# Attention products from block 6 on as 64x64 matmuls on the four quarters of TensorE's array, k and v loaded by head, orders written anew

## The chip, the cores and the metric

The kernel runs on one core of a Trainium2 chip. The metric is the device time of one execution in microseconds. Three runs of the kernel before took 210.29, 210.59 and 211.29 us; the median is 210.59 us.

## The reference

A chunked linear attention with a decay per head is followed by a feed-forward layer with a "snake" activation. There are 4 batches, 8 heads, 768 positions and 64 values per head; the feed-forward layer takes 3072 tokens of 512 values through 2048 hidden values. Cut to what matters:

```python
for b in range(nb):                                   # nb = 12 blocks of 64 positions
    intra = einsum('bhic,bhjc->bhij', qb, kb) * Dmask # Dmask[i,j] = lam**(i-j) for i >= j, else 0
    intra = einsum('bhij,bhjd->bhid', intra, vb)
    inter = einsum('bhid,bhde->bhie', qb * lam**(pos+1), kv_state)
    out[:, :, sl] = intra + inter
    kv_state = lam**64 * kv_state + einsum('bhsd,bhse->bhde', kb * lam**(63-pos), vb)
h = x @ w_in                                          # x: tokens x (heads * 64)
g = h + sin(alpha * h)**2 / (alpha + 1e-9)
return g @ w_out
```

## The kernel before

**Blocks.** The kernel works with 24 blocks of 128 positions, six to a batch (s = 0 to 23, n = s % 6). Decay is put into the operands: q is multiplied by lam to the position and k by lam to minus the position (scale_block, L460 to L501), so that one mask of ones and zeros is left for the products within a block, and the state of a batch is a plain running sum. Four blocks make a chunk c of 512 tokens of the feed-forward layer (xT[c], 6 chunks).

**One block of attention.** With two heads to a pair of 128 partitions, a block has four products on TensorE (PE): S, the scores of its keys and queries (part_S, L618); Z, the sum of k times v, which is accumulated in PSUM bank 7 over the whole batch (part_Z, L662 from block 6 on); the part of the output that comes from the state of earlier blocks (L713 for blocks 6 to 11, whose copy Zc holds the state alone; L700 for the others, whose copy Zd is block-diagonal and 128 by 128); and the output from the masked scores (L722). DVE masks the scores out of two banks into Sm (L629). ACT or DVE copies the state to Zc or Zd (L678, L672) and the output to xT (L732). piece_G(s, t) (L806) issues S of block s and the output and Z of block t as one piece of PE work. Blocks 0 to 3 use other functions (piece_P, piece_I).

**Inputs of a block.** load_kv (L351) loads k and v of one block with one DMA each, 128 positions on 128 partitions, all 8 heads, 256 KB; load_q (L327) loads q for two blocks, 512 KB. All are issued by SP. scale_block then makes bf16 copies (qk2, v2). For blocks below 8, PE transposes q and k (L516, L539); from block 8 on a DMA transpose does (L506), which SP issues too.

**Feed-forward.** unit_A (L828) and unit_A2 (L862) are the first product, one bank of 512 columns at a time; ACT takes the sine (L838, L872), POOL or ACT squares it (L843, L842), DVE adds (L845, L880) into gT. The second product is unit_B (L893) for chunk 0, and from chunk 1 on unit_P (L981), seven half-size products with sums of weights and tokens (L936, L959).

**What sets the order.** Every operation is recorded with an index and with what it reads and writes. A table written out by hand, _Plan.ORDER, gives for each engine (PE, ACT, DVE, POOL, SP) the indices in the order in which that engine runs them; an operation that may run on several engines runs on the one whose table holds it. Semaphore waits follow from the reads and writes. Every engine runs its list strictly in order.

Of the kernel before, what the change touches and what calls it, by code (L numbers as in the profile page):

```python
# [5 lines left out]
ALU = mybir.AluOpType  # L6
# [29 lines left out]
class _Plan:  # L36
# [16 lines left out]
        ),  # L53
        "ACT": (
# [161 lines left out]
def bass_lightning_attn__then__act_snake_kernel(  # L216
# [16 lines left out]
    NBLK = B * NB  # L233
    NM = DFF // 128
    NKC = DM // 128
    TCH = 512
    NCH = B * S // TCH
    BPC = TCH // BL

    RL = 6  # L240
    R2 = 6
    RT = 6
    TD = 8
    LB = 12
    SD = 12
# [12 lines left out]
    with es:  # L258
# [54 lines left out]
        def _(_unused_eng):  # L313
# [322 lines left out]
            def diag(s):  # L636
                return s < NB or s >= SD

# [616 lines left out]
```

## Time and profile before

| | |
|---|---|
| median of three runs | 210.59 us |
| span of the profiled execution, first to last instruction | 208.2 us |
| TensorE matmuls busy | 200.0 us, 96% |
| DVE, ACT, POOL busy | 168.5, 147.7, 132.4 us |
| moved by DMA | 34.40 MB in 83222 packets, 59632 of them under 512 B |

The page doesn't tell how long the profiled execution took outside its span. Beside the median of the runs, the span leaves 2.4 us for what lies ahead of the first and behind the last instruction. The chain of work that ended last lies to 79% on PE.

### The profile page before, as it was taken

What the parts mean: (1) busy time and instruction counts of PE and PEld (TensorE: products, weight loads), DVE (VectorE), ACT (ScalarE), POOL (GpSimd) and SP (SyncE); (2) the same over time, 40 slices, a digit from 0 to 9 for tenths busy, and PEclk for the clock granted to TensorE, in tenths of its full rate; (3) what the DMA queues carried; (4) which work ended last, traced back from release to release, by engine and by line L of the source; (5) the groups of instructions that cost most, each with busy time, mean ns of one, the idle gap of its engine ahead of it and who ended that gap; (6) DMA issues with size and microseconds to landing.
All of it is one profiled execution on the core that took longest, in us unless ns stands there. A gap on an engine that the chain in (4) does not pass through costs nothing.

```text
span 208.2 us, 4897 instructions
## 1 busy us (share of the span) xinstructions
PE 200.0 (96%) x1972; PEld 136.8 (66%) x1972; DVE 168.5 (81%) x296; ACT 147.7 (71%) x270; POOL 132.4 (64%) x140
## 2 busy tenths in 40 slices
PE   6988999999997999998999999999999999999995
PEld 6756444557765877665657576665667666667994
DVE  2898567886989999987988979899798866767854
ACT  5658999448998999976979776898765579734300
POOL 6065689834968987954796850958851695585400
DMA  4999999999899999799997999380300004000324
GB/s 133 323 315 216 202 255 214 213 238 245 197 179 230 232 250 248 154 215 206 208 245 156 242 271 185 67 194 26 136 0 3 0 32 169 3 0 20 128 94 165
DMA packets 83222, 34.40 MB, mean 165 GB/s; under 512 B 59632, under 2 KB 80384, under 8 KB 83200
## 3 DMA queue, kind: packets, MB, share of 16 engines
q1 hardware_dynamic: 78544, 29.24, 62.5%
q0 software_dynamic: 3696, 3.67, 10.9%
q10 hardware_dynamic: 960, 1.19, 1.9%
q8 instruction: 15, 0.25, 0.5%
q14 instruction: 7, 0.06, 0.1%
HBM read 27.28 MB, written 6.29 MB: 161 GB/s over the span
## 4 chain that ended last, share of the span: by engine, by line
PE 79%; DVE 9%; ACT 4%; DMA 3%; SPq 2%; issue 1%; ACTq 1%; POOL 0%
PE bank L828 28%; PE bank L981 26%; PE bank L862 7%; PE bank L893 6%; PE bank L722 3%; PE bank L618 3%; DMA v<-in_v_dram 3%; SPq L324 2%; DVE gT L880 2%; DVE Sm L629 2%; DVE gT L845 2%; PE bank L700 1%; DVE w L936 1%; PE bank L654 1%; ACT Zd L672 1%; PE bank L662 1%
## 5 line engine op out<-in xcount | busy, mean ns | idle before, releaser
L828 PE MATMUL bank<-xT,w 128*128 128x512 bf16 x296 | 70.9, 380 | 1.0 <-ACT kept L1018 0.7
L845 DVE SCALAR_TENSOR_TENSOR gT<-u,rinv,bank 128x512 bf16<-128x512 bf16 x74 | 53.6, 744 | 18.2 <-ACT u L842 14.1
L838 ACT ACTIVATE t<-bank,alpha 128x512 bf16<-128x512 f32 x74 | 49.9, 683 | 19.9 <-PE bank L828 19.0
L828 PEld LDWEIGHTS bank<-xT,w 128*128 128x128 bf16 x296 | 27.8, 98 | 28.8 <-DVE gT L845 1.4
L959 POOL TENSOR_TENSOR gT<-gT 128x512 bf16<-128x512 bf16 x28 | 32.1, 1158 | 14.1 <-DVE Xs L959 8.9
L842 ACT ACTIVATE u<-t 128x512 bf16<-128x512 bf16 x57 | 35.2, 628 | 1.5
L843 POOL TENSOR_TENSOR u<-t 128x512 bf16<-128x512 bf16 x17 | 17.6, 1040 | 25.7 <-ACT t L838 25.7
L629 DVE TENSOR_TENSOR Sm<-bank,mask 128x1024 bf16<-128x1024 f32 x24 | 28.9, 1216 | 3.0 <-PE bank L618 1.1
L862 PE MATMUL bank<-xT,w 128*128 128x256 bf16 x176 | 21.6, 273 | 1.0 <-DVE gT L880 1.0
L880 DVE SCALAR_TENSOR_TENSOR gT<-u,rinv,bank 128x256 bf16<-128x256 bf16 x44 | 18.9, 474 | 4.2 <-ACT u L876 3.5
L959 POOL TENSOR_TENSOR Xs<-gT 128x512 bf16<-128x512 bf16 x19 | 21.8, 1162 | 0.3 <-DVE gT L845 0.3
L981 PE MATMUL bank<-w,gT 128*128 128x256 bf16 (+1 forms) x168 | 20.1, 268 | 0.0
L872 ACT ACTIVATE t<-bank,alpha 128x256 bf16<-128x256 f32 x44 | 18.5, 471 | 2.0 <-PE bank L862 1.7
L981 PE MATMUL bank<-ws,gT 128*128 128x256 bf16 x160 | 19.6, 273 | 0.0
L981 PE MATMUL bank<-w,Xs 128*128 128x256 bf16 (+1 forms) x168 | 19.5, 268 | 0.0
L478 POOL TENSOR_TENSOR qk<-q,Lq 128x512 bf16<-128x512 f32 x17 | 18.2, 1077 | 2.0 <-DMA q<-in_q_dram 2.0
L497 POOL TENSOR_TENSOR qk<-k,Lk 128x512 bf16<-128x512 f32 x16 | 17.4, 1090 | 3.3 <-DMA k<-in_k_dram 3.2
L862 PEld LDWEIGHTS bank<-xT,w 128*128 128x128 bf16 x176 | 16.3, 98 | 4.2 <-DVE gT L880 1.8
L981 PEld LDWEIGHTS bank<-w,gT 128*128 128x128 bf16 x168 | 15.9, 98 | 4.1 <-DVE gT L959 0.2
L981 PEld LDWEIGHTS bank<-w,Xs 128*128 128x128 bf16 x168 | 15.6, 98 | 3.3
L981 PEld LDWEIGHTS bank<-ws,gT 128*128 128x128 bf16 x160 | 15.3, 98 | 3.1 <-ACT xT L732 0.4
L893 PE MATMUL bank<-w,gT 128*128 128x512 bf16 x64 | 15.8, 380 | 0.0
(105 smaller groups left out, 266.0 us busy)
## 6 DMA issues: line engine op xcount, KB each, us to landing
k<-in_k_dram SPq DMA_DIRECT2D x24, 256.0 KB, 5.1
q<-in_q_dram SPq DMA_DIRECT2D x12, 512.0 KB, 6.2
v<-in_v_dram SPq DMA_DIRECT2D x24, 256.0 KB, 5.8
out_dram<-osb SPq DMA_DIRECT2D x18, 256.0 KB, 2.6
w<-in_moe_w_out_dram POOLq DMA_DIRECT2D x4, 512.0 KB, 7.8
w<-in_moe_w_in_dram POOLq DMA_DIRECT2D x3, 512.0 KB, 8.1
ws<-in_moe_w_in_dram SPq DMA_DIRECT2D x2, 512.0 KB, 7.5
out_dram<-osb ACTq DMA_DIRECT2D x8, 128.0 KB, 3.7
```

Of the source, the lines that this page charges most:

```text
L478: lambda e, a=a: e.tensor_tensor(qk2[:, j:j + 2, 4 * a:4 * a + 4, :], q32[:, jq, 4 * a:4 * a + 4, :, :].rearrange("p h t d -> p t h d"), b ...
L629: op("DVE", lambda e: e.tensor_tensor(Sm[js][:, :, :], banks[:, 512 * b0:512 * b0 + 1024].rearrange("p (c i) -> p c i", i=128), bass.AP(ma ...
L828: ins = e.matmul(ps[hb][:, c0:c1], w1[:, kc, 128 * m:128 * (m + 1)], xT[x][:, kc, c0:c1], start=(kc == 0 and c0 == lo), stop=(kc == NKC - ...
L838: op("ACT", lambda e: e.activation(t16[ju][:, w], ps[hb][:, w], ACTF.Sin, scale=alpha[:, m:m + 1]), 0.69 if hi - lo == TCH else 0.475, [ba ...
L842: lambda e: (e.activation(u16[ju][:, w], t16[ju][:, w], ACTF.Square) if e is nc.scalar else e.tensor_tensor(u16[ju][:, w], t16[ju][:, w], ...
L845: op("DVE", lambda e: e.scalar_tensor_tensor(out=gT[g][:, m, w], in0=u16[ju][:, w], scalar=rinv[:, m:m + 1], in1=ps[hb][:, w], op0=ALU.mul ...
L862: ins = e.matmul(ps[hb][:, 256 * i:256 * i + 256], w1[:, kc, 128 * (m + i):128 * (m + i + 1)], xT[x][:, kc, lo:lo + 256], start=(kc == 0 a ...
L872: op("ACT", lambda e, i=i: e.activation(t16[ju][:, 256 * i:256 * i + 256], ps[hb][:, 256 * i:256 * i + 256], ACTF.Sin, scale=alpha[:, m + ...
L880: op("DVE", lambda e, i=i: e.scalar_tensor_tensor(out=gT[g][:, m + i, lo:lo + 256], in0=u16[ju][:, 256 * i:256 * i + 256], scalar=rinv[:, ...
L893: ins = e.matmul(ps[ob][:, w], gT[g][:, m, 128 * s4:128 * (s4 + 1)], w2[:, m, w], start=(m == 0), stop=(m == NM - 1),)
L959: e.tensor_tensor(dst, in0, in1, alu), 0, rd, wr))
L981: ins = e.matmul(ps[ob][:, lo + d0:lo + d1], lhs, rhs[:, d0:d1], start=first and p == 0, stop=(p == NM // 2 - 1), skip_group_check=True)
```

## The change

**Products.** From block 6 on (NL = 6) piece_G calls a new function, quarters(s, t, ob), in place of part_S, part_O and part_Z. Every matmul in it has 64 rows and 64 columns of weights. The four quarters of the array are named by the half of the partitions that a matmul reads (rows) and the half of the partitions of PSUM that it writes (columns); four matmuls that follow each other go to four different quarters. Keys are cut into two halves of 64 positions; the second half meets only the second 64 queries, so its matmuls have 64 columns in place of 128.

Up to three pieces of PE work come out of one call. The first ("begun") is half of the product with the state. The second ("mid") is the scores of block s and the state's new term of block t. The third ("end") is the rest of the product with the state and the output of block t. Scores and the state's term lie in banks 1 and 2, the output in banks 7 and ob, one for each half of rows.

**Around the products.** The state is no longer kept in PSUM: DVE adds each block's term to an fp32 copy in SBUF (Zs), and ACT, DVE or POOL casts that to Zc. The masked scores have 768 columns in place of 1024, with a mask of their own (mlate). The output goes to xT in two copies of 256 columns in place of one of 512.

**Loads.** From block 6 on, k and v come by head: a DMA for three blocks of one head, 64 positions on 64 partitions, 6 times 64 values each (96 KB); heads 0, 1, 4 and 5 lie on the lower half of the partitions, the others on the upper half. The factors of k (Lk) are made anew for that layout, with two iotas and two small multiplies more at the start; the new mask takes four affine selects.

**Orders.** All five tables of ORDER are new; of PE's, a line before and after:

```diff
-            235, 244, 225, 236, 240, 251, 264, 248, 249, 272, 320, 257, 283, 278, 270, 293, 321, 289, 308, 302,
+            254, 269, 280, 277, 278, 293, 301, 286, 356, 312, 299, 307, 325, 357, 318, 319, 344, 338, 350, 331,
```

```diff
+    NL = 6
-    SD = 12
...
             def load_kv(s, which="kv"):
                 b, n, j = s // NB, s % NB, s % RL
                 for nm, src, dst in (("k32", k, k32), ("v32", v, v32)):
-                    if nm[0] not in which or (s < NP and s % 2):
+                    if nm[0] not in which or (s < NP and s % 2) or (s >= NL and s % 3):
                         continue
...
+                    for h in range(H):
+                        half, jp, par = h // 4, h // 2 % 2, h % 2
+                        at = H * D * j + D * (2 * par + half)
+                        load(
+                            bass.AP(dst, 64 * jp * RL * H * D + at, [[RL * H * D, 64], [4 * D, 6], [1, D]]),
+                            src[b, h, n * BL:(n + 3) * BL, :].rearrange("(c p) d -> p c d", p=64),
+                            [(nm, j + i, h) for i in range(3)], 0.45, f"{nm}{j}u", lat=1.5,
+                        )
...
+            def quarters(s, t, ob):
+                xy = (XB, ob)
+                n = 0 if t is None else t % NB
...
+                def inter(e, same):
...
+                    for par in range(2):
+                        for half in range(2):
+                            jp = half if same else 1 - half
+                            ins = mm(e, ("o", jp), half, par,
+                                     ps[xy[jp]][rows(par), 128 * half:128 * half + 128].rearrange("p (t x) -> p t x", t=2),
+                                     Zc[(t - 1) % 2][rows(half), 2 * jp + par, :], qkT[rows(half), jq:jq + 2, 2 * jp + par, u])
...
+                def scores(e):
...
+                    for c in range(2):
+                        x = slice(u.start + 32 * c, u.stop)
+                        for par in range(2):
+                            at = 640 + 192 * par + 64 * (1 - c)
+                            for half, jp in ((0, 0), (1, 1), (0, 1), (1, 0)):
...
+                def state(e):
...
+                    for c in range(2):
+                        for par in range(2):
+                            for jp, half in ((0, 0), (1, 1), (0, 1), (1, 0)):
+                                i = 4 * c + 2 * par + half
+                                lo = 512 + 896 * jp + 64 * par
+                                ins = mm(e, ("s", jp), jp, half, banks[rows(half), lo:lo + 64],
+                                         qk2[rows(jp), j, H + i, :], v2[rows(jp), j, i, :])
...
+                def outputs(e):
...
+                    for c in range(2):
+                        for half in range(2):
+                            for jp, par in ((0, 0), (1, 1), (0, 1), (1, 0)):
...
+                if t is not None and n:
+                    begun = op("PE", lambda e: inter(e, False), 0.06, qT(t) + [("Zc", (t - 1) % 2)], obank)
...
+                    op("PE", mid, 0.3, (qT(s) + [("kT", s % RT)] if s is not None else []) + (kv if z else []),
+                       [bank(1), bank(2)])
...
+                    o = op("PE", end, 0.25, kv + [("Sm", t % 2)] + (qT(t) + [("Zc", (t - 1) % 2)] if n else []), obank)
...
+                if s is not None:
+                    op("DVE", lambda e: e.tensor_tensor(
+                        sm(s).rearrange("p (g i) -> p g i", i=192),
+                        banks[:, 640:1408].rearrange("p (g i) -> p g i", i=192),
+                        bass.AP(mlate, 0, [[192, 128], [0, 4], [1, 192]]), ALU.mult), 0.95,
...
+                    if n:
+                        op("DVE", lambda e: e.tensor_tensor(zs, zp, zs, ALU.add), 0.43, [bank(1), bank(2), "Zs"], ["Zs"])
...
+                    op(ADP, lambda e: (e.copy if e is nc.scalar else e.tensor_copy)(Zc[t % 2][:, :, :], Zs[:, :, :]), 0.35,
+                       ["Zs"], [("Zc", t % 2)])
...
             def piece_G(s, t, ob=3):
-                run(None if s is None else part_S(s, 1, 2),
-                    None if t is None else part_O(t, ob), None if t is None else part_Z(t))
+                if (t if s is None else s) < NL:
+                    run(None if s is None else part_S(s, 1, 2),
+                        None if t is None else part_O(t, ob), None if t is None else part_Z(t))
+                else:
+                    quarters(s, t, ob)
```

The first place is PE in the third batch, where one block's attention stands between products of the feed-forward layer. A row gives the line, the operation, the tiles, the shape of the moving operand and the count. Before (L828 and L981 are the feed-forward products):

```order
L828 MATMUL bank<-xT,w 128x512 x4
L700 MATMUL bank<-qkT,Zd 128x128 x4
L618 MATMUL bank<-qkT 128x128 x8
L722 MATMUL bank<-Sm,v 64x128 x8
L662 MATMUL bank<-v,qk 64x64 x8
L828 MATMUL bank<-xT,w 128x512 x4
```

In the changed kernel the same place on PE (L975 and L1128 are the feed-forward products, L833 is the one line of all quarters):

```order
L975 MATMUL bank<-xT,w 128x512 x4
L833 MATMUL bank<-qkT,Zc 64x128 x4
L833 MATMUL bank<-qkT 64x128 x8
L833 MATMUL bank<-qkT 64x64 x8
L833 MATMUL bank<-v,qk 64x64 x16
L833 MATMUL bank<-qkT,Zc 64x128 x4
L833 MATMUL bank<-Sm,v 64x128 x8
L833 MATMUL bank<-Sm,v 64x2x32 x8
L1128 MATMUL bank<-w,Xs 128x256 x8
```

28 matmuls became 56, and all of them are of one kind. There are 22 such uninterrupted groups from block 6 on, where there were 21.

The second place is SP from its first load behind the wait for the weights on. Before, with k and v in blocks of 256 KB and q in 512 KB; by the table's indices these are q, k and v of block 4, k of 7, v of 5, q of 6, k of 9, v of 6 and k of 6:

```order
L324 DMA q<-in_q_dram 128x8x128
L324 DMA k<-in_k_dram 128x8x64
L324 DMA v<-in_v_dram 128x8x64
L324 DMA k<-in_k_dram 128x8x64
L324 DMA v<-in_v_dram 128x8x64
L324 DMA q<-in_q_dram 128x8x128
L324 DMA k<-in_k_dram 128x8x64
L324 DMA v<-in_v_dram 128x8x64
L324 DMA k<-in_k_dram 128x8x64
```

In the changed kernel the rows on SP from block 5's v on (ahead of them stand q, k and v of block 4 and four loads by head of k); the loads 64x6x64 are those by head, eight of k and eight of v for blocks 6 to 8:

```order
L334 DMA v<-in_v_dram 128x8x64
L334 DMA k<-in_k_dram 64x6x64
L334 DMA q<-in_q_dram 128x8x128
L334 DMA k<-in_k_dram 64x6x64 x2
L334 DMA v<-in_v_dram 64x6x64
L334 DMA k<-in_k_dram 64x6x64
L334 DMA v<-in_v_dram 64x6x64
L334 DMA q<-in_q_dram 128x8x128
L334 DMA k<-in_k_dram 64x6x64
L334 DMA v<-in_v_dram 64x6x64 x6
```

The eighth k of blocks 6 to 8 now stands behind the q of block 6, and the eighth v behind one q more (block 8) and one load of k of blocks 9 to 11. Up to there 3.9 MB have been asked for; before, up to v of block 6, 2.5 MB.

The third place is PE where the quarters begin (L1009 and L1040 are feed-forward, L559 the transposes of k). In the changed kernel:

```order
L833 MATMUL bank<-qkT 64x128 x8
L833 MATMUL bank<-qkT 64x64 x8
L559 MATMUL bank<-ident,qk 128x128 x4
L1009 MATMUL bank<-xT,w 128x256 x8
L1040 MATMUL bank<-w,gT 128x512 x4
L833 MATMUL bank<-qkT 64x128 x8
L833 MATMUL bank<-qkT 64x64 x8
L833 MATMUL bank<-v,qk 64x64 x16
L833 MATMUL bank<-Sm,v 64x128 x8
L833 MATMUL bank<-Sm,v 64x2x32 x8
```

The scores of block 7 and the state's term of block 6 are one piece there, so that piece waits for v of block 6; before, the scores of block 7, the output and Z of block 6 were one piece, which waited for it in the same way.

More of the change, by code (lines that the diff above doesn't have):

```diff
@@ L349, in pair32, with slot @@
                 return t[:, H * D * (j + a):H * D * (j + a + 1)].rearrange("p (h t d) -> p h t d", t=2, d=D)
+            def slot(nm, j):
+                return [(nm, j, h) for h in range(H)]
             def load_kv(s, which="kv"):
@@ L413, in _ @@
                                         channel_multiplier=2), 0.6, writes=["E_i"])
[L414 to L416 removed]
+            op("POOL", lambda e: e.iota(E_i[:, NB:NB + 4, :], [[1, 4], [0, H]], base=0, channel_multiplier=4),
                0.5, writes=["E_4"])
[L418 removed]
+            op("POOL", lambda e: e.iota(E_i[:, NB + 4:NB + 6, :], [[128, 2], [0, H]], base=128 * NP, channel_multiplier=1),
+               0.5, writes=["E_k"])
+            for jp in range(2):
+                part = op("POOL", lambda e, jp=jp: e.iota(
+                    E_i[64 * jp:64 * jp + 64, NB + 6:2 * NB + 6, :], [[64, 2 * NB], [0, H // 2]], base=0,
+                    channel_multiplier=1), 0.6, writes=[("E_l", jp)])
+                part.some = True
+            op("POOL", lambda e: e.tensor_copy(E_f[:, :, :], E_i[:, :, :]), 0.3,
+               ["E_i", "E_k", "E_4", ("E_l", 0), ("E_l", 1)], ["E_f"])
             op("DVE", lambda e: e.memset(idle, 1.0), 0.2, writes=["idle"])
@@ L433, in _ @@
                     part.some = i < 2
+            op("DVE", lambda e: e.memset(mlate[:, :], 1.0), 0.2, writes=[("mlate", 0), ("mlate", 1)])
+            for jp in range(2):
+                for lo, x in ((0, 32), (64, 64)):
+                    part = op("POOL", lambda e, jp=jp, lo=lo, x=x: e.affine_select(
+                        out=mlate[64 * jp:64 * jp + 64, lo:lo + 2 * x], in_=mlate[64 * jp:64 * jp + 64, lo:lo + 2 * x],
+                        pattern=[[1, 2], [2, x]], compare_op=ALU.is_ge, fill=0.0, base=0, channel_multiplier=-1), 0.3,
+                       [("mlate", jp)], [("mlate", jp)])
+                    part.some = True
             for i in range(2):
@@ L540, in mm @@
                         return ins
-                    op("PE", mm, 0.23, [("q2", j, a), ("q2", j + 1, a), "ident"], [bank(tbs[a % len(tbs)])])
+                    op("PE", mm, 0.23, [("q2", j + t, i) for t in range(2) for i in ((a,) if s < NL else range(2))] + ["ident"],
+                       [bank(tbs[a % len(tbs)])])
                     if len(tbs) == 2:
@@ L708, in mm @@
                     ins = None
-                    if n and not wide:
-                        for jp in range(4):
-                            for h in range(2):
-                                r = slice(64 * h, 64 * h + 64)
-                                e.matmul(
-                                    ps[obs[jp // 2]][r, 128 * jp:128 * (jp + 1)].rearrange("p (t x) -> p t x", t=nq),
-                                    Zc[(s - 1) % 2][r, jp, :], qkT[r, jq:jq + nq, jp, u],
-                                    start=(jp in new), stop=False, skip_group_check=True,
-                                )
                     for t, i in enumerate(sm):
```

169 lines of the change are left out of this document (115 added, 54 removed), and 114 rows, old and new, of the table ORDER.

## The prediction

> **What bounds the kernel now.** First I read the page for the engine with the least idle time, then PE's waits, then the two stages in which the change lies.
>
> ```profile
> span 208.2 us, 4897 instructions
> PE 200.0 (96%) x1972; PEld 136.8 (66%) x1972; DVE 168.5 (81%) x296; ACT 147.7 (71%) x270; POOL 132.4 (64%) x140
> ```
>
> PE is busy for 96% of the span, with DVE next at 81%. PE's waits from 17 us on (who waited, for whom, total us, times, longest; the three left out are shorter):
>
> ```profile
> PE bank L862 <- DVE gT L880: 1.0, 1, 1.0
> PE bank L828 <- ACT kept L1018: 0.7, 1, 0.7
> ...
> ```
>
> The two longest waits make 1.7 us. So PE sets the end, and PE work that goes shortens the kernel unless something else comes late in its place. The two stages with attention from block 6 on, with each engine's busy time (PE, PEld, DVE, ACT, POOL), clock, DMA share and GB/s:
>
> ```profile
> 52.00:83.00 31.00, 29.94 (x366) 22.36 (x364) 29.73 (x59) 28.67 (x62) 25.62 (x25) 1.00 1.15 222
> 83.00:150.00 67.00, 66.00 (x636) 43.24 (x636) 59.35 (x96) 54.01 (x93) 47.12 (x46) 1.00 0.84 180
> ```
>
> Between 52 and 83 us DVE is as full as PE (29.7 and 29.9 of 31 us) and DMA moves 222 GB/s without a pause. After 83 us DVE is at 89%. Whatever the change gains before 83 us has two near neighbours.
>
> **PE work removed.** Attention of one block in the third batch and of one in the second (start, duration, operation; the next row's start is what counts, since durations hold the tail of a pipelined matmul):
>
> ```profile
> 132.15 1.03 PE L828 MATMUL bank<-xT,w 128*128 128x512 bf16 x4
> 133.01 0.39 PE L700 MATMUL bank<-qkT,Zd 128*128 128x128 bf16 x4
> 133.33 0.40 PE L618 MATMUL bank<-qkT 64*128 64x128 bf16 x8
> 133.66 0.41 PE L722 MATMUL bank<-Sm,v 128*64 128x128 bf16 x8
> 133.90 0.29 PE L662 MATMUL bank<-v,qk 128*64 128x64 bf16 x8
> 134.13 0.39 PE L828 MATMUL bank<-xT,w 128*128 128x512 bf16 x1
> ...
> 70.21 0.40 PE L618 MATMUL bank<-qkT 64*128 64x128 bf16 x8
> 70.54 0.41 PE L713 MATMUL bank<-qkT,Zc 64*64 64x128 bf16 x8
> 70.88 0.41 PE L722 MATMUL bank<-Sm,v 128*64 128x128 bf16 x8
> 71.12 0.29 PE L662 MATMUL bank<-v,qk 128*64 128x64 bf16 x8
> 71.35 0.28 PE L981 MATMUL bank<-ws,gT 128*128 128x256 bf16 x1
> ```
>
> The first takes 134.13 - 133.01 = 1.12 us, the second 71.35 - 70.21 = 1.14 us. In PE's order, blocks 6 to 23 stand in 21 groups: 8 of the first kind (8.96 us), 3 of the second (3.42), one each of the first and second without scores and Z (0.66 and 0.68), one of the first without Z (0.99), one of the second without scores (0.81), 3 without the state's product (0.33 + 0.24 + 0.23, so 2.4 in all) and 3 of scores alone (0.99). That is 18.9 us. Eleven of them begin with a product on half the rows, and entering one costs 0.11 us, as the next rows show: 1.2 us more. **Before: 20.1 us.**
>
> **PE work added.** The kernel already has 64x64 matmuls on all four quarters, in blocks 0 to 3:
>
> ```profile
> 14.08 0.60 PE L1140 MATMUL bank<-Xs 128*128 128x512 bf16 x2
> 14.62 0.42 PE L618 MATMUL bank<-qkT 64*64 64x128 bf16 x16
> 14.97 0.62 PE L654 MATMUL bank<-v,qk 64*128 64x128 bf16 x8
> 15.52 0.64 PE L765 MATMUL bank<-Sm,v 64*64 64x128 bf16 x32
> 16.09 0.23 PE L785 MATMUL bank<-qkT,Zd 128*128 128x128 bf16 x1
> ```
>
> 16 of them take 14.97 - 14.62 = 0.35 us and 32 take 0.57 us. So each costs 0.22 / 16 = 13.75 ns, four at once, and a change of tile shape 0.13 us behind. Ahead, two matmuls of 512 columns take 0.54 us where four at 132.15 take 0.86, so entering costs 0.11. One uninterrupted group of quarters thus pays 0.24 us, whatever is in it, where a block before changed shape three or four times.
>
> The changed kernel has from block 6 on 408 quarter matmuls of 128 columns (8 of scores and 8 of output in 18 blocks, 8 with the state in 15) and 528 of 64 columns (8 and 8 in 18 blocks, 16 for the state's term in 15), in 22 groups. The 408 cost 5.6 us and the 22 groups 5.3 us. A quarter matmul of 64 columns isn't in the trace. It costs between 6.9 ns (half of 13.75) and 13.75 ns (no shorter than at 128 columns). L662, on halves with 64 columns, takes 0.23 us for 8, so 0.10 without the 0.13 behind: 12.5 ns on two tiles, and L722 at 128 columns 0.24 for 8: 30 ns. Halving the columns there halved the time at least, so I take a value near the low end, 7.5 ns: 4.0 us. **After: 14.9 us**, and 5.2 us saved. With 6.9 ns it is 5.5, with 13.75 ns 1.9 us.
>
> The Trainium skill, "TensorE: Matmul & The Clock Gate", section "Wait — 56ns, not 53.3ns?", says that the start-to-start time of matmuls never falls below about 25 ns, however few the columns. The 13.75 ns of the rows above differ: on four quarters the trace goes below that. At 25 ns for the 528 alone the sum would rise by 9.2 us; as a mechanism it is the third rival.
>
> **Waits added: data.** The rows here are the page's on loads of k; the stages in which blocks 6 to 9 are loaded; SP's issue of v for block 6 and for block 9; landing times of the loads issued from 44 to 57 us; and the use of v in block 6 (that in block 9 stands at 70.88 above).
>
> ```profile
> k<-in_k_dram SPq DMA_DIRECT2D x24, 256.0 KB, 5.1
> ...
> 44.00:57.00 13.00, 13.00 (x133) 8.93 (x132) 10.93 (x20) 10.59 (x23) 8.79 (x10) 1.00 0.98 219
> 57.00:70.00 13.00, 11.94 (x142) 8.90 (x140) 12.37 (x23) 11.64 (x27) 10.13 (x10) 1.00 1.16 210
> ...
> 40.17 3.57 SPq L324 DMA_DIRECT2D v<-in_v_dram  x1
> 50.66 2.56 SPq L324 DMA_DIRECT2D v<-in_v_dram  x1
> ...
> DMA to landing us min/median/max: 4.3/5.5/7.7
> ...
> 55.30 0.41 PE L722 MATMUL bank<-Sm,v 128*64 128x128 bf16 x8
> ```
>
> DMA is full here, so a load lands when the bytes ahead of it are through. Before, v of block 6 has 2.5 MB of SP's up to it and lands by 40.17 + 7.7 = 47.9 us at the latest; it is needed at 55.30. Now all three blocks must be there: 3.9 MB, 1.4 MB later, at 219 GB/s 6.4 us: 54.3 us, and it has still to be cast. That is a wait between nothing and some 1 us. For block 9 it was 4.5 MB and by 58.4 us, and becomes 6.6 MB with three DMA transposes between: 2.1 MB at 210 GB/s is 10 us, so 68.4 us and up to 2 us more for the transposes, against a need at 70.88 less some 1.5 us gained by then. Again 0 to 1.5 us. Behind a waiting matmul stands all of PE's list, so such a wait counts in full. The bounds are 0 and 3 us; I take **1.5 us**, the middle. It is paid once: later batches' loads stand further ahead of their use, since DMA falls from 222 to 180 GB/s.
>
> **SP.** 60 more loads are issued:
>
> ```profile
> 85.01 2.60 SPq L506 DMA_TRANSPOSE qkT<-qk  x2
> 87.66 0.58 SPq L324 DMA_DIRECT2D k<-in_k_dram  x1
> ```
>
> From 57 to 140 us SP's table holds 72 loads by head and 16 transposes: at 0.58 and 1.3 us, 63 of 83 us. That fits; were each load 0.85 us, SP would be full.
>
> **DVE.** Groups of DVE (busy, mean ns, idle before):
>
> ```profile
> L629 DVE TENSOR_TENSOR Sm<-bank,mask 128x1024 bf16<-128x1024 f32 x24 | 28.9, 1216 | 3.0 <-PE bank L618 1.1 <-PE bank L722 1.0 <-PE bank L654 0.9
> L732 DVE CAST xT<-bank 128x512 bf16<-128x512 f32 x8 | 5.9, 735 | 1.2 <-PE bank L662 1.0 <-PE bank L722 0.2
> L678 DVE CAST Zc<-bank 128x256 bf16<-128x256 f32 x2 | 0.8, 420 | 0.2 <-PE bank L662 0.2
> ```
>
> A mask over 768 columns lies midway between 735 and 1216 ns: 0.98 us, so 18 of them save 4.3 us. Fifteen sums of the state at 0.42 add 6.3. By the tables DVE gives up 11 of 12 copies to Zd or Zc and takes 6 from Zs (-2.1), and does 11 xT copies of 0.42 in place of 8 of 0.735 (-1.3). Sum: -1.4 us, and eleven token sums move to POOL besides. DVE gets no fuller, but beside a PE that is 2 us shorter between 52 and 83 us it stays full; the 1.5 us hold that too.
>
> **Start.** Lp, which releases the first multiply of k, waits for ACT's table:
>
> ```profile
> 4.09 1.28 ACT L440 ACT_TABLE_LOAD   x1
> 5.68 0.23 ACT L445 ACTIVATE Lp<-lnL 128x32 f32<-128x32 f32 x1
> 4.11 0.29 DVE L441 TENSOR_TENSOR lnL<-E_f,lnlam 128x128 f32<-128x128 f32 x1 [2.36 <-ACT lnlam L438]
> ```
>
> Two small multiplies of at most 0.29 us stand ahead of lnL now, which ends by 5.0 instead of 4.4 us, and two iotas on POOL delay it by some 0.4. The table load covers both up to 5.68; I count nothing. Without that cover it would be 1 us.
>
> **Sum.** 208.2 - 5.2 + 1.5 = 204.5 us of span. The page doesn't give the execution's time outside its span; with 2.4 us, the distance to the median of 210.6 us, it is **206.9 us**, 1.8% less.
>
> **Rivals.** (1) *Half of the gain only*: 64 columns cost 13.75 ns, so 1.9 us are saved and the waits take 1.5 of them: 210.2 us. For it: nothing in the trace shows four quarters at 64 columns. Against: L662.
>
> (2) *Data late, slower than before*: a load by head writes only half of the partitions. At 219 GB/s its 96 KB take 0.45 us. Were it limited by the half it writes, it could take up to 0.9 us, and 32 of them stand up to v of block 9. Each 0.1 us costs PE 3.2 us there, less about 1 us of slack. From 0.65 us on (6.4 - 1 = 5.4) the change's gain is gone. At 0.75 us PE waits 8.6 us: 210.6 - 5.2 + 8.6 = 214 us. For it: DMA is full there and three blocks wait for the last of 16 loads. Against: heads of both halves are in flight together. The Trainium skill, "SBUF — State Buffer", section "Door 1: The DMA port swizzle", says that partitions 0 to 63 reach only half of the DMA ports. Its full rate of about 435 GB/s halves to 218, an estimate from that page, which is what the trace moves anyway: by that rule a load by head would take 0.45 us still.
>
> (3) *No overlap beyond two tiles at 64 columns*: as long as L662's 0.23 / 8 = 29 ns each, the 528 take 15.3 us instead of 4.0, and the kernel takes 206.9 + 11.3 = 218 us. The 25 ns of the page above would come to 216.
>
> That the quarters don't run side by side at all is excluded by the 13.75 ns.
>
> **How the numbers follow.** Forecast 0.62 (204.5 to 209.4 us), rival 1 0.13, rival 2 0.20, rival 3 0.03; 0.02 are for DVE holding the stage from 52 to 83 us at its old length beside late data (211 to 212 us). A measurement of this kernel can tell about 0.5% from no change, 1.05 us. Faster is the forecast and a small part of rival 1: 0.64. Same is nearly all of rival 1: 0.12. Slower is the rest: 0.24. The low end takes 5.5 us saved and no wait, and the two old waits of 1.7 us partly gone: 204.2. The high end goes to rival 2 at 0.75 us: 214.0.
>
> **What would show it.** A block's attention of about 0.8 us between feed-forward products, start to start, with the 64-column matmuls at 7 to 8 ns each; 13 ns or more means rival 1 or 3. PE's waits: none for casts of v or k over 1.5 us between 50 and 75 us; a wait of several us there, with loads by head landing late, is rival 2. DVE's mask near 0.98 us. The forecast is wrong as well if PE loses more than 3 us to waits after 83 us, for which I see no cause.

## The result, and the profile after

The changed kernel takes **222.93 us** (median of 4 runs, 222.66 to 224.97), the kernel before 210.87 us beside it: a ratio of 1.061 (1.056 to 1.066). The forecast was 206.9 us and a range up to 214.0 us. It was wrong. Here and below, medians are of all runs of a kernel, while ratios and their intervals leave out runs over 1.5% above its fastest. The profiled execution took 222.66 us, 2.1 us more than its span.

The page's first lines (span; busy time of each engine) answer to those of before, 208.2 us with PE 200.0 us busy:

```profile
span 220.6 us, 5863 instructions
PE 197.5 (90%) x2395; PEld 134.9 (61%) x2420; DVE 177.7 (81%) x306; ACT 146.0 (66%) x272; POOL 151.3 (69%) x160
```

PE does less, as forecast, and yet it is busy for only 90% of the span. The two stages of before, now (same columns):

```profile
52.00:83.00 31.00, 27.62 (x500) 21.16 (x501) 28.40 (x57) 27.41 (x63) 23.31 (x23) 1.00 0.94 171
83.00:150.00 67.00, 56.77 (x759) 37.71 (x767) 56.65 (x96) 43.89 (x78) 49.88 (x48) 0.97 0.90 189
```

PE lacks 3.4 and 10.2 us in them, where it lacked 1.1 and 1.0. Between 52 and 83 us DMA moves 171 GB/s in place of 222: the data come more slowly, though DMA has room (its share is 0.94, where 1.15 was reached before). What PE waits for from 17 us on:

```profile
PE bank L833 <- DMA qkT<-qk: 3.7, 4, 2.2
PE bank L975 <- DVE gT L1027: 2.5, 2, 2.1
PE bank L1009 <- DVE gT L1027: 2.4, 2, 1.3
PE bank L582 <- POOL qk L521: 2.3, 1, 2.3
PE bank L833 <- DVE v L543: 1.5, 2, 1.0
```

No single wait explains 12 us; PE waits for transposed q and k, for DVE and for POOL. Two of them cost twice. Behind the waits at 36.5 and 134.9 us the clock granted to PE was halved:

```profile
37.20:40.60 3.40, 3.40 (x10) 1.22 (x9) 1.16 (x1) 1.37 (x2) 3.38 (x4) 0.50 1.34 197
136.20:139.60 3.40, 3.07 (x55) 1.68 (x54) 2.71 (x6) 0.88 (x3) 3.40 (x4) 0.50 0.86 258
```

Each stretch lasts 3.41 us and costs up to 1.7 us, so up to 3.4 us of PE's 197.5 are not work. The work is some 194 us where it was 200: 5 to 6 us were saved. One block's attention with scores, state and output, but without a product with the state, shows the price of the quarters:

```profile
58.64 0.81 PE L1040 MATMUL bank<-w,gT 128*128 128x512 bf16 x3
59.38 0.37 PE L833 MATMUL bank<-qkT 64*64 64x128 bf16 x16
59.58 0.30 PE L833 MATMUL bank<-v,qk 64*64 64x64 bf16 x16
59.71 0.34 PE L833 MATMUL bank<-Sm,v 64*64 64x128 bf16 x16
59.98 1.26 PE L1009 MATMUL bank<-xT,w 128*128 128x256 bf16 x10
```

From start to start 0.60 us for all of it, and 0.13 us for the 16 matmuls of 64 columns: 8 ns each. A block with all 56 matmuls takes 0.71 us where nothing in it waits:

```profile
161.68 0.25 PE L833 MATMUL bank<-qkT,Zc 64*64 64x128 bf16 x4
...
162.40 1.05 PE L1128 MATMUL bank<-w,gT 128*128 128x256 bf16 x8
```

**Where the time went** is on an engine that does no arithmetic. Here are the DMAs that SP issues between 57 and 140 us, in groups (count; shortest, median and longest issue in ns), and some of SP's rows (start, us, DMA):

```profile
L334 SPq DMA_DIRECT2D v<-in_v_dram x38: 599/627/1394, 59.7 to 138.8; - x38
L334 SPq DMA_DIRECT2D k<-in_k_dram x35: 596/626/1527, 57.0 to 133.7; - x35
L334 SPq DMA_DIRECT2D q<-in_q_dram x6: 542/622/1562, 59.1 to 139.5; - x6
...
L549 SPq DMA_TRANSPOSE qkT<-qk x12: 1286/1785/3125, 61.0 to 131.7; - x12
```

```profile
95.51 4.09 SPq L549 DMA_TRANSPOSE qkT<-qk  x2
99.64 5.84 SPq L334 DMA_DIRECT2D v<-in_v_dram  x7
105.53 1.58 SPq L334 DMA_DIRECT2D k<-in_k_dram  x2
107.22 1.29 SPq L549 DMA_TRANSPOSE qkT<-qk  x1
```

Each row starts where the one before ends. Added up, the 95 DMAs of these 83 us (with 4 stores of outputs) are 79.4 us of issuing, and 0.04 us stand between two of them: SP is full. It is so from 24 to 146 us: among 127 DMAs the longest gap is 0.45 us. Before, SP was 58.3 us busy in the same 83 us, and its rows show gaps:

```profile
91.09 1.11 SPq L324 DMA_DIRECT2D k<-in_k_dram  x1
95.20 3.83 SPq L506 DMA_TRANSPOSE qkT<-qk  x2
```

Here 3 us lie between 92.20 and 95.20. That SP holds the data up, and not the other way round, one input of block 18 shows. Its q goes into the buffer of q of block 12, which POOL has read by 67.31 us (rows of POOL, SP and PE in the order of time):

```profile
64.77 2.54 POOL L521 TENSOR_TENSOR qk<-q,Lq 128x512 bf16<-128x512 f32 x2
...
118.36 0.62 SPq L334 DMA_DIRECT2D q<-in_q_dram  x1
...
123.23 2.22 POOL L521 TENSOR_TENSOR qk<-q,Lq 128x512 bf16<-128x512 f32 x2 [2.34 <-DMA q<-in_q_dram]
126.53 1.04 POOL L540 TENSOR_TENSOR qk<-k,Lk 128x512 bf16<-128x512 f32 x1
...
128.50 4.47 SPq L549 DMA_TRANSPOSE qkT<-qk  x2
...
134.89 0.36 PE L833 MATMUL bank<-qkT 64*64 64x128 bf16 x14 [2.18 <-DMA qkT<-qk]
```

The load could have been issued 51 us earlier; behind it POOL waits, then the transpose stands in SP's queue for 0.9 us more, and PE waits. By the program's dependences, every load by head found its buffer free for at least 3 us when SP came to it, half of them for over 20 us, and every transpose up to 146 us found its data ready.

### The profile page after: what moved, and what is told of

It is laid out like the page before. It is cut to its first block, busy times and chain, and to the rows that moved or that the text cites. A ratio compares the mean times of both kernels' runs of the same rounds, so it can differ in the third digit from the quotient of the medians.

```text
span 220.6 us, 5863 instructions
## 1 busy us (share of the span) xinstructions
PE 197.5 (90%) x2395; PEld 134.9 (61%) x2420; DVE 177.7 (81%) x306; ACT 146.0 (66%) x272; POOL 151.3 (69%) x160
## 4 chain that ended last, share of the span: by engine, by line
PE 47%; DMA 19%; DVE 13%; POOL 10%; SPq 7%; issue 2%; ACT 2%; ACTq 0%; POOLq 0%
PE bank L1128 19%; PE bank L975 16%; DMA q<-in_q_dram 7%; SPq L334 6%; PE bank L1040 5%; DVE gT L1027 4%; DMA w<-in_moe_w_in_dram 4%; DMA qkT<-qk 4%; DMA v<-in_v_dram 3%; PE bank L833 3%; POOL qk L521 3%; PE bank L1009 2%; POOL gT L1106 2%; POOL qk L540 2%; DVE Sm L927 2%
## 5 line engine op out<-in xcount | busy, mean ns | idle before, releaser
L975 PE MATMUL bank<-xT,w 128*128 128x512 bf16 x278 | 69.8, 388 | 5.1 <-DVE gT L1027 2.5
L992 DVE SCALAR_TENSOR_TENSOR gT<-u,rinv,bank 128x512 bf16<-128x512 bf16 x74 | 53.8, 740 | 13.8 <-ACT u L989 10.2
L975 PEld LDWEIGHTS bank<-xT,w 128*128 128x128 bf16 x296 | 28.2, 99 | 31.3 <-DVE gT L1027 3.3
L1106 POOL TENSOR_TENSOR gT<-gT 128x512 bf16<-128x512 bf16 x34 | 40.2, 1188 | 10.0 <-DVE gT L992 4.4
L1106 POOL TENSOR_TENSOR Xs<-gT 128x512 bf16<-128x512 bf16 x24 | 28.7, 1205 | 8.7 <-DVE gT L992 4.9
L990 POOL TENSOR_TENSOR u<-t 128x512 bf16<-128x512 bf16 x17 | 18.3, 1077 | 9.9 <-ACT t L985 9.7
L1009 PE MATMUL bank<-xT,w 128*128 128x256 bf16 x176 | 21.6, 273 | 2.4 <-DVE gT L1027 2.4
L1128 PE MATMUL bank<-w,gT 128*128 128x256 bf16 (+1 forms) x168 | 20.6, 268 | 0.0
L1009 PEld LDWEIGHTS bank<-xT,w 128*128 128x128 bf16 x176 | 16.3, 98 | 6.0 <-DVE gT L1027 3.3
L927 DVE TENSOR_TENSOR Sm<-bank,mlate 128x768 bf16<-128x768 f32 x18 | 17.0, 947 | 3.7 <-PE bank L833 3.7
L1128 PE MATMUL bank<-w,Xs 128*128 128x256 bf16 (+1 forms) x168 | 20.0, 268 | 0.0
L1128 PE MATMUL bank<-ws,gT 128*128 128x256 bf16 x160 | 19.9, 273 | 0.0
L1128 PEld LDWEIGHTS bank<-w,Xs 128*128 128x128 bf16 x168 | 15.7, 98 | 3.7
L1128 PEld LDWEIGHTS bank<-w,gT 128*128 128x128 bf16 x168 | 15.3, 98 | 3.9 <-DVE gT L1106 0.5
L1128 PEld LDWEIGHTS bank<-ws,gT 128*128 128x128 bf16 x160 | 15.6, 98 | 3.3 <-DVE osb L1174 0.2
L944 ACT CAST xT<-bank 128x256 bf16<-128x256 f32 x25 | 10.7, 446 | 10.3 <-PE bank L833 10.0
```

The costliest lines, as they stand in the source:

```text
L927: op("DVE", lambda e: e.tensor_tensor(sm(s).rearrange("p (g i) -> p g i", i=192), banks[:, 640:1408].rearrange("p (g i) -> p g i", i=192), ...
L975: ins = e.matmul(ps[hb][:, c0:c1], w1[:, kc, 128 * m:128 * (m + 1)], xT[x][:, kc, c0:c1], start=(kc == 0 and c0 == lo), stop=(kc == NKC - ...
L992: op("DVE", lambda e: e.scalar_tensor_tensor(out=gT[g][:, m, w], in0=u16[ju][:, w], scalar=rinv[:, m:m + 1], in1=ps[hb][:, w], op0=ALU.mul ...
L1009: ins = e.matmul(ps[hb][:, 256 * i:256 * i + 256], w1[:, kc, 128 * (m + i):128 * (m + i + 1)], xT[x][:, kc, lo:lo + 256], start=(kc == 0 a ...
L1106: e.tensor_tensor(dst, in0, in1, alu), 0, rd, wr))
L1128: ins = e.matmul(ps[ob][:, lo + d0:lo + d1], lhs, rhs[:, d0:d1], start=first and p == 0, stop=(p == NM // 2 - 1), skip_group_check=True)
```

## The experiments

Theory: **SP's queue is the bound** (C). Rivals: (A) the order at the start, where POOL issues the second load of w_out 7.6 us earlier than before, ahead of q of block 4; (B) between 61 and 89 us DVE is the bound, since its sums stretch while POOL works. A half of (C) had its own rival: the loads land late because of how they write, or since three blocks wait for one group. Each time is a median beside runs of the kernel before (210.3 to 210.7 us) on the same chip.

### The order at the start

In POOL's table of the changed kernel (113 to 116 are the loads of w_out), and the reverse in the kernel before:

```diff
-112, 215, 113, 114, 149, 158, 165, 169, 173, 185, 29, 31, 32, 115,
+112, 215, 113, 149, 158, 165, 169, 173, 185, 29, 114, 31, 32, 115,
```

> The changed kernel, with the second load of w_out put back behind the squares of feed-forward units on POOL (to where it stood before, next to a mask select). Theory A (that load, issued 7.6 us earlier than before, puts 0.5 MB ahead of q of block 4; PE then waits 2.35 us at 36.5 us and its clock is halved for 3.4 us): q of block 4 lands near 31.5 us, no PE wait over 0.5 us before 50 us, no halved clock there, 4 us less: 219 us. Theories B (DVE and POOL collide between 61 and 89 us) and C (96 loads by head fill SP's queue and come late) alone: 222 to 223 us, since what is gained early is lost at the next late load.

> The kernel of before, with only the second load of w_out moved right behind the first on POOL, ahead of five squares of feed-forward units, as the changed kernel has it. Theory A: q of block 4 lands 2 to 3 us later, PE waits 2 us for its scaling near 33 us and its clock is halved for some 3.4 us: 4 us more, 214.6 us. If the order of these loads is not the cause: 210.9 us, within 1 us.

The changed kernel with the load late: **223.03 us** (220.7 to 225.2; ratio 1.056, 1.047 to 1.065), so no gain that these runs show, and not the 4 us. The kernel before with the load early: 211.66 us (1.006, 1.003 to 1.009), 1.3 us lost in place of 4; PE waited 1.9 us there, and its clock wasn't halved. In the first, PE's waits read

```profile
PE bank L833 <- DMA qkT<-qk: 7.1, 5, 3.3
PE bank L559 <- DVE qkT L593: 2.9, 1, 2.9
```

q of block 4 landed at 31.4 us as expected. But DVE now waited for that load of w_out, with the copies of q behind it. So its sums of weights were moved too (DVE's table):

```diff
-202, 190, 212, 365, 363, 236, 210, 206, 238, 198, 244, 368,
+202, 190, 212, 236, 210, 206, 238, 198, 244, 365, 363, 368,
```

> The changed kernel with the second load of w_out put back as in the first experiment, and with DVE's two first sums of weights, which wait for that load, put behind the copies of q and k of block 4 and the mask of block 4 (before had them behind those too). Theory A': the load was not the cause alone, since the sums that DVE does in order ahead of those copies wait for it: no PE wait over 0.6 us between 30 and 50 us, no halved clock there, and the start of block 4's attention 3 to 4 us earlier. The total then falls by 3 to 4 us, to 219 to 220 us, if what follows keeps its distance, and stays at 222 to 223 if a later load takes it back, as in the first experiment.

**223.49 us** (1.058, 1.053 to 1.064): again nothing, though only 1.9 us of waits for w_out were left near 40 us.

```profile
PE bank L832 <- DMA qkT<-qk: 7.8, 4, 4.3
PE bank L1039 <- DMA w<-in_moe_w_out_dram: 1.9, 2, 1.5
```

In both runs the waits for transposed q and k rose from 3.7 us to 7.1 and 7.8. In the first, the gain at 40 us was gone at once, to PE's wait of 2.9 us for DVE. In the second, PE was 3.4 us ahead of the changed kernel at 40 us (by the times at which both finish the same operation) and 1.5 us ahead from 46 to 57 us. Then POOL waited 2.24 and 1.30 us for loads of v and q, and by 68 us PE was behind. What is won early is handed back where the kernel next meets SP's queue. Theory A names a true wait that sets nothing here.

### DVE beside POOL

```diff
+for x, i in enumerate((370, 372, 399, 410, 467, 489, 490, 491, 510, 533, 538, 539, 548)):
+    P.ops[i].emit = lambda e, x=x: e.tensor_copy(junk[:, x:x + 1], identf[:, 0:1])
```

> The changed kernel with 13 of POOL's instructions between 64 and 90 us (two sums of weights, two token sums, squares of two units, the scaling of q of blocks 12 and 14 and of k of blocks 12 to 14, a cast of v) replaced by a copy of one column, so that those results are left out: some 17 us less for POOL there, nothing else changed. Theory B (DVE's sums and casts within SBUF stretch while POOL works): DVE's sums of weights go from 1.6 us to 0.7, its token sums from 0.68 us to near 0.41, its casts from 0.66 to 0.28, and of PE's 5.4 us of waits for DVE between 64 and 92 us at most 1.5 remain. Rival (DVE has too much work of its own there, POOL has no part in it): the durations stay and so do the waits.

**222.67 us** (1.059, 1.054 to 1.064): nothing again. The mechanism is there, though. Groups of DVE from 61 to 92 us (busy, mean ns) in the changed kernel:

```profile
L1083 DVE TENSOR_TENSOR w<-w 128x1024 bf16<-128x1024 bf16 x2 | 3.3, 1638 | 0.0
L1106 DVE TENSOR_TENSOR Xs<-gT 128x512 bf16<-128x512 bf16 x4 | 3.3, 836 | 0.0
L1106 DVE TENSOR_TENSOR gT<-gT 128x512 bf16<-128x512 bf16 x4 | 2.8, 722 | 0.0
```

and with POOL emptied (its lines stand one further down):

```profile
L1107 DVE TENSOR_TENSOR Xs<-gT 128x512 bf16<-128x512 bf16 x4 | 1.6, 417 | 0.0
L1107 DVE TENSOR_TENSOR gT<-gT 128x512 bf16<-128x512 bf16 x4 | 1.6, 416 | 0.0
...
L1084 DVE TENSOR_TENSOR w<-w 128x1024 bf16<-128x1024 bf16 x2 | 1.4, 678 | 0.0
```

The same instructions take half the time without POOL's work beside them; only the casts to Zc stayed at 0.70 us. The Trainium skill, "SBUF — State Buffer", section "Who interferes with whom", says that a DVE instruction with two inputs in SBUF contends with a GpSimd instruction that reads SBUF; the fall from 836 to 417 ns agrees. DVE won 4.8 us, and PE's waits for transposes rose to 6.3 us. SP's queue was untouched. The clock took a share too: of PE's waits from 17 us on (16.9 us in the changed kernel) 12.3 are left, but there are four stretches at half clock in place of two, up to 3.4 us more. So that SP alone ate the gain isn't shown.

### The loads by head

Merged two by two, at the place of the earlier (the even head's operation is shown; the other issues nothing):

```diff
-bass.AP(dst, 64 * jp * RL * H * D + at, [[RL * H * D, 64], [4 * D, 6], [1, D]]),
-src[b, h, n * BL:(n + 3) * BL, :].rearrange("(c p) d -> p c d", p=64),
+bass.AP(dst, 64 * jp * RL * H * D + at, [[RL * H * D, 64], [2 * D, 12], [1, D]]),
+src[b, h, :, :].rearrange("(c p) d -> p c d", p=64),
```

> The changed kernel, with its loads by head merged two by two: 48 DMAs of 192 KB on a partition half in place of 96 of 96 KB, each at the place of the earlier of the two, a block still waiting for all loads of its group. (The rows of each are those of one head's whole sequence, so the output is another one; bytes, partitions and descriptors are the same.) SP then issues 32 us less. Theory C by the number of issues: 4 to 6 us less, 217 to 219 us. If what counts in theory C is that three blocks wait for the last of a group: within 1.5 us of 222.9. Theories A and B: the same, within 1.5 us.

**217.42 us** (1.033, 1.028 to 1.039): 5.5 us less with half of the issues, the same bytes and partitions, and the group's wait still there. Then as blocks:

```diff
-for h in range(H):
-    load(bass.AP(dst, ...), src[b, h, ...], [(nm, j + i, h) for i in range(3)], ...)
+    load(block32(dst, j + i), src[b, :, (n + i) * BL:(n + i + 1) * BL, :].rearrange("h p d -> p h d"),
+         slot(nm, j + i), 1.18, f"{nm}{j + i}", lat=2.7)
```

> The changed kernel, but from block 6 on k and v come one block at a time over all 128 partitions, as before, at the places of the third, sixth and eighth load by head of each group: 36 loads in place of 96, the same bytes, none earlier, and a block waits for its own load alone. The data then lie on the wrong partitions, so the output is another one; all products, sums and scalings are those of the changed kernel. Theory C (loads by head): the waits after 88 us go, some 6 us of them with one halved clock, 216 us. Theories A and B: they keep what is before 89 us, so at most 1.5 us less, 221.5 to 223 us.

**214.34 us** (1.020, 1.013 to 1.028): 8.6 us less, the largest step of all. In the profiled execution, of 212.54 us, no stretch with a halved clock is left. The other three (213.5 to 215.7 us) were granted 0.991 or 0.992 of the clock over their spans, which comes to one stretch each. SP has gaps again, as at 96.64 and 102.1 us:

```profile
94.34 2.30 SPq L334 DMA_DIRECT2D v<-in_v_dram  x2
99.58 1.28 SPq L554 DMA_TRANSPOSE qkT<-qk  x1
100.90 1.19 SPq L334 DMA_DIRECT2D v<-in_v_dram  x1
103.30 2.01 SPq L554 DMA_TRANSPOSE qkT<-qk  x1
```

This run also lets a block go on with its own load. To part that from SP's time:

```diff
-slot("k32", jl) + ["Lk"]
+[("k32", jl // 3 * 3 + i, h) for i in range(3) for h in range(H)] + ["Lk"]
```

(and the same for v).

> The kernel with block loads, but the scaling of k and the cast of v of a block wait for the loads of all three blocks of its group, and the next loads into the group's slots for all three, as with loads by head; so 36 issues on 128 partitions with the group's wait. If the group's wait is a price of its own: 217 us, as with the merged loads (48 issues on half partitions). If only SP's time counts: 214.3 us, within 1 us.

**215.31 us** (1.020, 1.012 to 1.028), the same ratio as without the wait: waiting for the whole group costs nothing that these runs tell. What counts is SP's time.

### The same price in the kernel before

There the loads were only cut up:

```diff
-e.dma_start(block32(dst, j), src[b, :, n * BL:(n + 1) * BL, :] ...)
+[e.dma_start(block32(dst, j)[p0:p1, h0:h1, :], ...) for p0, p1, h0, h1 in parts]
 # by heads:  parts = (0, 128, 0, 3), (0, 128, 3, 6), (0, 128, 6, 8)
 # by halves: parts = (0, 64, 0, 8), (64, 128, 0, 4), (64, 128, 4, 8)
```

> The kernel of before, with each load of k and v from block 6 on issued as three DMAs by heads (3, 3 and 2 heads, all 128 partitions): 108 issues in place of 36, the same bytes at the same places, nothing else changed. Theory C1 (SP's issues are the price: 72 more at 0.6 us are 43 us of SP): loads and transposes behind them come later, 3 to 6 us more, 214 to 216 us. Theory C2 (what costs is that three blocks wait for one group, or the half partitions, in an order that leaves no slack): within 1 us of the kernel before.

> The same, but the three DMAs of each load write half of the partitions each (rows 0 to 63 of all heads; rows 64 to 127 of heads 0 to 3; the same of heads 4 to 7): also 108 issues, the same bytes. If writing one half of the partitions is slower by itself (the prediction's second rival), this is at least 2 us slower than the split by heads and its loads land later; if only issues count, the two are within 1 us of each other.

By heads **215.87 us** (1.025, 1.019 to 1.031), 5.2 us more; by halves of the partitions **226.72 us** (1.069, 1.059 to 1.078), by the ratios some 9 us more again. Here my reading of the rival has to be split. SP's loads from 57 to 140 us, first by heads, then by halves (count; shortest, median, longest issue):

```profile
L366 SPq DMA_DIRECT2D k<-in_k_dram x41: 444/488/1527, 56.5 to 131.0; - x41
L366 SPq DMA_DIRECT2D v<-in_v_dram x39: 378/489/1552, 59.2 to 137.5; - x39
```

```profile
L366 SPq DMA_DIRECT2D k<-in_k_dram x39: 605/622/1575, 57.8 to 139.5; - x39
L366 SPq DMA_DIRECT2D v<-in_v_dram x35: 595/617/1537, 56.5 to 129.2; - x35
```

A DMA that writes 64 partitions takes SP 0.62 us to issue in the median, one that writes 128 partitions 0.49 us, whatever its size here (64 to 128 KB). The DMA ahead counts too: q, on 128 partitions, took 0.61 us in the median right behind a load by halves and 0.47 right behind one by heads. Over the 108 loads that write half of the partitions, the 0.13 us between the two medians are 14 us of SP. Their data don't come later: the page's medians from issue to landing are 2.7 to 3.0 us by halves and 2.6 to 3.0 us by heads. So half partitions do have a price, but SP pays it. With SP nearly full already, 14 us of issuing became some 9 us of time. Why the issue takes longer, no run shows.

### Loads on ACT, and what is left

```diff
 [(nm, j + i, h) for i in range(3)], 0.45, f"{nm}{j}u", lat=1.5,
+eng="ACT" if len(P.ops) in P.ORDER["ACT"] else "SP",
```

> The changed kernel, with 35 of its 96 loads by head issued by ACT instead of SP (4 of each group, fewer where ACT is full), each at a place in ACT's order where its slot was free in the changed kernel's trace. Same loads, same bytes, same data. Theory SP (SP issues without a gap from 24 to 146 us, its queue is the bound): SP gets 23 us less to issue, has gaps again after 83 us, and the kernel takes 215 to 218 us although ACT gets 21 us more. Rival (loads by head come late because of how they write, or since three blocks wait for one group): 222 to 224 us, with ACT's extra work on top.

It moved 38 loads, not 35. **219.82 us** (1.041, 1.034 to 1.047): 3.1 us less than the changed kernel with the same loads, the right direction and short of the 215 to 218 expected. SP has gaps again after 83 us, as here at 92.30 us,

```profile
91.67 0.63 SPq L333 DMA_DIRECT2D q<-in_q_dram  x1
93.44 4.14 SPq L549 DMA_TRANSPOSE qkT<-qk  x2
```

but ACT issues most of them at 0.60 to 0.66 us each, 24.5 us in all, in a list on which PE waits too. The rest of the difference to the merged loads I put down to that; it wasn't measured apart.

The next two add to this the two edits of the start, and then (DVE's and POOL's tables):

```diff
-DVE:  334, 336, 369, 335, 342, 343, 355, 354, 371, 406
+DVE:  334, 336, 335, 342, 343, 355, 354, 406
-POOL: 490, 489, 370, 409, 372, 410
+POOL: 490, 489, 369, 370, 409, 371, 372, 410
```

> The same, and besides the second load of w_out and DVE's first sums of weights put late, as in the run that did this alone and gained nothing (223.5). Theory SP: what is gained early was eaten by SP's queue there; with SP relieved it stays, so 2 to 3 us less than the kernel with a third of the loads on ACT alone. Rival: no difference to that, within 1 us.

> The same, and besides DVE's two sums of weights at 64 and 68 us (1.24 and 2.04 us) done by POOL. Theory B (between 61 and 89 us DVE is the bound once SP isn't): 1 to 2 us less again. Rival (ACT is the bound there by now, with the loads it issues): no difference, or more.

221.69 us (1.053, 1.048 to 1.058) and 224.39 us (218.42 to 226.04). The first is no better than the run before it, against the expectation. The second scatters too widely for a verdict. In both, PE now waits longest for the cast of v of block 6 on POOL (4.5 and 3.7 us near 63 us), and POOL for that load (4.6 us in the second): a new wait that the loads issued by ACT ahead of it may have caused. No run parts that, and the two traces are of executions of 226.62 and 226.04 us, well above the medians.

The last two start from the block loads (214.34 us), one with the table edits of the start and of the two sums of weights, the other with POOL emptied as above:

> The kernel with block loads in place of loads by head (214.3; its data lie on the wrong partitions, so the output is another one), with the second load of w_out and DVE's first sums of weights late and the two later ones on POOL. If the quarters save 5 us of PE as forecast and the rest of the loss is the early stage (2 to 4 us) and DVE from 61 to 89 us (1 to 3 us): 207 to 210 us, not above the kernel before. If the quarter products themselves cost more than their records show: 213 us or more.

> The kernel with block loads in place of loads by head (214.3 us; data on the wrong partitions), and besides the 13 instructions of POOL between 64 and 90 us replaced by copies of one column, as in the run that emptied POOL and gained nothing with SP full. Theory B as second bound (with SP relieved, DVE's stretched sums set the stage from 61 to 89 us): PE's 3.3 us of waits there go and the kernel takes 2 to 4 us less, 210 to 212 us. Rival (the stage's pace is set by transposes and loads still): within 1 us of 214.3.

Tuned: 212.32 us (1.011, 1.005 to 1.017), short of 207 to 210. POOL emptied: **211.90 us** (1.008, 1.004 to 1.011). So emptying POOL, worth nothing with SP full, is worth 2.4 us once SP is relieved. That fits theory B as a second bound behind the first: PE's 2.8 us of waits for gT from DVE, the longest with block loads, are no longer among the longest. But POOL's own work on q, k and v went as well, and no run parts it from DVE's stretched sums. The longest waits of PE from 17 us on are now:

```profile
PE bank L565 <- DVE qkT L599: 2.0, 1, 2.0
PE bank L588 <- POOL qk L527: 1.8, 1, 1.8
PE bank L1134 <- DVE osb L1180: 1.7, 2, 1.4
```

The first two are the waits of the start, at 35 to 45 us, the third cause. No version that computes the reference's output beat the kernel before.

## Why the prediction was wrong, by its own steps

**PE work** (5.2 us saved): right. 5 to 6 us were saved, a 64-column matmul on four quarters costs 8 ns (taken: 7.5), and a block where nothing waits 0.71 us, with the 0.11 us of entering it the 0.8 that was said. Rivals 1 and 3 are out.

**SP** ("63 of 83 us; that fits"): the step that failed. It counted 72 loads at 0.58 us and 16 transposes at 1.3 us. Those 83 us held 73 loads by head at 0.68 us on average (49.5 us), only 12 transposes at 1.91 us (23.0), 6 loads of q (4.7) and 4 stores (2.3), which I left out, and the gaps between them, mostly 0.04 us each (4.6): 84.0 us, the last one ending 1.0 us behind the stage. Of the 21.5 us or so that my list (62.6 us) lacked, q and the stores are 7.0, the gaps 4.6, the longer loads 7.7 and the longer transposes 2.2, although four of these had been pushed out of the stage by then. My 0.58 us was the issue of one block on 128 partitions; a load by head on 64 takes 0.63 in the median and up to 1.5. My own limit, "were each load 0.85 us, SP would be full", was off for the same reason. And a queue that is just full is not harmless until it overflows: it also runs late by whatever it lacked before, here from 29 us on.

**Waits added: data** (1.5 us, between 0 and 3): wrong by its mechanism. At the two places where it looked for the wait, block 6 has none and block 9 has 0.5 us (at 77.17 us, for the cast of v); the waits grew later. It asked how many bytes stand ahead of a load in DMA, where it should have asked how many issues stand ahead of it on SP. The group's wait, on which the term rests, costs nothing measurable (215.3 beside 214.3 us). "Later batches' loads stand further ahead of their use" is the opposite of what the rows at 118.36 and 134.89 us show.

**DVE** ("gets no fuller"): the prices were right (mask 0.95 us for 0.98, sum of the state 0.41 for 0.42), the sum was not: 177.7 us busy for 168.5. I moved eleven token sums to POOL as a relief and didn't see that DVE's sums stretch beside POOL's work. How much of the 9.2 us more is that stretch, no run parts. Under SP's bound POOL's work between 64 and 90 us cost nothing that the time shows; without it, 2.4 us.

**Start**: two things were missed. PE's wait for Zd stands at 19.27 us where it stood at 18.81; some 0.5 us went into the stage that the added iotas and small multiplies lengthen. And POOL's order of the loads of w_out, part of the new tables, wasn't read at all; it made the wait of 2.35 us at 36.5 us.

**Rival 2** (data late, slower than before) had the right sign, and one number fits by luck: "from 0.65 us on the change's gain is gone", and a load by head takes 0.67 us from start to start in the median, but on SP. It looked for the price in the landing of the bytes, priced 32 loads where all 96 count, and so ended at 214 us. "More than 3 us of waits after 83 us, for which I see no cause" came true with more than 9.

The Trainium skill, "Perfetto Trace Analysis", section "What "DMA-bound" means", names this case: the issuing engine's sequencer is solid with DMA slices. The trace agrees, 127 DMAs with gaps of 0.04 us. It goes on that large descriptors are what matters then. Here all variants load k and v in the same runs of 256 bytes, and it was the number of DMAs that counted, 5.2 us more with 72 more of them, and the partitions that each writes.

The sum, by these runs: 210.4 us before, less some 6 us of PE work, is 204.4. 211.9 us is what is left with block loads and POOL emptied: 7.5 us more, of which 4.2 us are PE's waits between 35 and 45 us in that trace; no run took those away without making others. 2.4 us more are POOL's work and DVE beside it (214.3), and 8.6 us the loads by head (222.9), up to 3.4 us of these through the halved clock: two stretches, where the runs with block loads have none or one. So the step on SP makes 8.6 of the 16.0 us between forecast and result, and without it the range, up to 214.0 us, would still have been missed, if barely. What stays open is the rest of the 7.5 us: waits of 0.2 to 1.4 us at many places of the new orders.

## What to carry to other kernels

Add up each queue's issues over a stage as you would an engine's instructions: every kind of DMA in it, from start to start, at the price of its own shape, beside the length of the stage; a queue without gaps can be the bound even where the DMA engines have room. When a gain at one place brings nothing, see which wait grew by the same amount elsewhere, and relieve that one first; a second cause can only be measured once the first is out of the way. To find what a queue costs, cut the old kernel's transfers up at the same bytes: that shows the price without the change.

## What the hardware showed that was not expected

In the two kernels with cut loads, the issue of a DMA of 64 to 128 KB cost SP by the partitions that it writes, not by its bytes: 0.62 us in the median for 64 of them, 0.49 us for 128; and a DMA right behind one on 64 partitions took 0.61 us though it wrote 128. DVE's sums of two bf16 operands in SBUF go from 417 to 836 ns in the mean while POOL works. And a wait need not be long to halve PE's clock: 2.35 us at 36.5 us was followed by 3.41 us at half clock in the changed kernel, while a wait of the same length at the same place was not in the one with block loads.
